# Long convolution beside a gated MLP: evictions issued one operation at a time between chunks, and a new spread of the chunks over the convolution's stages

## The chip, the cores and the metric

The kernel runs on one core of one Trainium2 chip. The metric is the device time of one execution in microseconds (us), the median of several runs. Comparisons use runs of the fast state. Engines are named as in the profile: PE is TensorE, PEld its weight loads, DVE VectorE, ACT ScalarE, POOL GpSimd, SP the queue that issues DMAs.

## The reference, cut to what matters

```python
# x, v: (4, 12480, 128); w_in: (128, 2048); w_out: (2048, 128); all float32
h_filt = (np.maximum(pos_emb @ w1, 0.0) @ w2) * np.exp(-0.01 * pos)[:, None]
u = x * v
y = irfft(rfft(u, n=2*S) * rfft(h_filt, n=2*S), n=2*S)[:, :S, :]    # along the sequence
z = (x * y).reshape(4 * 12480, 128)
h = z @ w_in
out = (h * np.cos(h)) @ w_out
```

## The kernel before

The FFTs are products with small DFT matrices. One sequence's convolution has five stages: **u** (product x*v, then sum and difference of mirrored rows, into the SBUF array `slots`; 30 units, no matmul), **f1** (first DFT factor, 64 units), **f2** (second factor and product with the filter, 48 units), **i1** (inverse, 64 units) and **i2** (30 units, times x, out to DRAM). The first sequence is convolved ahead (633 us, with the filter); the other three are convolved beside the MLP of the sequence before.

The MLP goes in *chunks*: 128 hidden columns for 480 tokens. A chunk is one up matmul, four element operations and one down matmul, spread over the engines (tile allocations are cut):

```python
    def moe_up(pool, n, c):                     # chunk i
        nc.tensor.matmul(ph[:, 0:TOK], w_in_sb[...], ats[n][:, :], start=True, stop=True)
        nc.scalar.activation(a, ph, AF.Identity, bias=quarter, scale=INV_TWO_PI)      # a
        nc.vector.tensor_scalar(out=k, in0=a, scalar1=ROUND, scalar2=ROUND, ...)      # k
        nc.gpsimd.tensor_tensor(f, a, k, op=ALU.subtract)                             # f
    def moe_act(pool, ph, f):                   # chunk i - 1
        nc.scalar.activation(cs, f, AF.Sin, scale=TWO_PI)                             # cs
        nc.vector.tensor_tensor(gt, ph, cs, op=ALU.mult)                              # gt
    def moe_down(n, c, gt):                     # chunk i - 4
        nc.tensor.matmul(accs[n][:, 0:TOK], w_out_sb[:, c, :], gt[:, :], ...)
    # ... cut ...
            owed += share                       # after each chunk, in the "gap":
            while owed > 0.0:                   # convolution work for `share` steps
                owed -= next(conv, owed)
```

The matmuls write to PSUM. Beside the MLP the program divides it into eight banks: two for `acc`, four for `ph`, **two for the convolution** (`cv`). FIFO (first in, first out) below means that an engine takes its instructions in the order in which they were issued. The convolution's units are issued by one generator; `steps` says for how many chunks a unit has to last, and `share` is the sum of steps over 380 chunks:

```python
    def units(n, steps, before, mm, after, ahead=2):
        # ... cut: loads ahead ...
        last = None
        for j in range(n):
            # ... cut ...
            now = mm(j)                  # takes a bank, issues the unit's matmuls
            if last is not None:
                after(j - 1, last)       # takes out the results of the unit before
            last = now
            yield steps
        after(n - 1, last)
        yield REST

    U_STEPS, F1_STEPS, F2_STEPS, I1_STEPS, I2_STEPS = 2.1, 1.2, 2.3, 1.2, 1.6

    def f1_evict(ps, b):
        pj = ps[:, 0:4 * N1].rearrange("p (i r k) -> p r k i", i=2, r=2)
        nc.scalar.copy(out=parts[0:ODD, :, :, b, :], in_=pj[0:ODD])
        nc.vector.tensor_copy(out=parts[ODD:KE, 0, :, b, :], in_=pj[ODD:KE, 1])
        nc.vector.tensor_scalar(out=parts[ODD:KE, 1, :, b, :], in0=pj[ODD:KE, 0],
                                scalar1=-1.0, scalar2=None, op0=ALU.mult)
    # i1_evict: one ScalarE copy, two VectorE operations; f2_product: four VectorE
    # multiplies from PSUM and two GpSimd additions; u: one product, one sum, one difference
```

Of the kernel before, what the change touches and what calls it, by code (L numbers as in the profile page):

```python
# [30 lines left out]
def kernel(  # L31
# [62 lines left out]
    UA = 2  # L94
# [174 lines left out]


# [57 lines left out]
    def u_multiply(tiles, engine):  # L328
        xt, vt = tiles
        engine.tensor_tensor(xt[:, :, :], xt[:, :, :], vt[:, :, :], op=ALU.mult)  # L330
# [9 lines left out]
    def f1_mm(ps, u, b):  # L340

        for i in range(2):
            nc.tensor.matmul(ps[0:KE, i * 2 * N1:(i + 1) * 2 * N1], u[:, b, 0:KE, i],  # L343
                             c1[0:u.shape[0], :, :].rearrange("p r k -> p (r k)"),
                             start=True, stop=True)

    def f1_evict(ps, b):
        pj = ps[:, 0:4 * N1].rearrange("p (i r k) -> p r k i", i=2, r=2)
        nc.scalar.copy(out=parts[0:ODD, :, :, b, :], in_=pj[0:ODD])
        nc.vector.tensor_copy(out=parts[ODD:KE, 0, :, b, :], in_=pj[ODD:KE, 1])  # L350
        nc.vector.tensor_scalar(out=parts[ODD:KE, 1, :, b, :], in0=pj[ODD:KE, 0],
                                scalar1=-1.0, scalar2=None, op0=ALU.mult)

    def f2_mm(ps, w, k1):

        for i in range(2):
            nc.tensor.matmul(ps[0:N2, i * 2 * D:(i + 1) * 2 * D], w[:, i, :],  # L357
                             parts[0:KE, :, k1 + i, :, :], start=True, stop=True)

    def f2_product(pool, ps, h, k1):  # L360
# [5 lines left out]
        for r, op in ((0, ALU.subtract), (1, ALU.add)):  # L366
            nc.vector.tensor_tensor(y[:, r], uu[:, 0], hh[:, r], op=ALU.mult)
            nc.vector.tensor_tensor(t[:, r], uu[:, 1], hh[:, 1 - r], op=ALU.mult)  # L368
            nc.gpsimd.tensor_tensor(y[:, r], y[:, r], t[:, r], op=op)  # L369

    def filter_keep(pool, ps, h, k1):

        uu = ps[0:N2, :].rearrange("p (g r d) -> p g r d", g=2, r=2)
        for g in range(2):
            k = slice(k1 + g, k1 + g + 1)
            nc.scalar.activation(h[:, g, :, :], uu[:, g, :, :], AF.Copy, scale=rot[:, 0, k])
            for r in range(2):
                nc.vector.scalar_tensor_tensor(
                    out=h[:, g, r, :], in0=uu[:, g, 1 - r, :], scalar=rot[:, 2 - r, k],
                    in1=h[:, g, r, :], op0=ALU.mult, op1=ALU.add)  # L380
        nc.sync.dma_start(hd[k1 // 2, :, :, :, :], h[:, :, :, :])

    def i1_mm(ps, b):
        for i in range(2):
            for r in range(2):
                nc.tensor.matmul(  # L386
                    ps[0:N1, (i * 2 + r) * N2:(i * 2 + r + 1) * N2],
                    parts[0:N2, r, :, b, i],
                    cs[:, r:r + 2, :].rearrange("p c a -> p (c a)"), start=True, stop=True)

    def i1_evict(pool, ps, b):
# [3 lines left out]
        for h, op in ((0, ALU.add), (1, ALU.subtract)):  # L395
            nc.vector.tensor_tensor(slots[0:N1, b, h * N2:(h + 1) * N2, :], pj[:, 0],  # L396
                                    other[:, :, :], op=op)

    def i2_mm(ps, t, g):
        for i in range(G):  # L400
# [9 lines left out]
    def i2_out(pool, ps, xs, b, g):  # L410
# [4 lines left out]
        nc.sync.dma_start(zd[b, :, g * G:(g + 1) * G, :], zs[:, :, :])  # L415

# [3 lines left out]
    def units(n, steps, before, mm, after, ahead=2):  # L420
        for j in range(min(ahead, n)):
            before(j)
        last = None
        for j in range(n):
            if j + ahead < n:
                before(j + ahead)
            now = mm(j)
            if last is not None:
                after(j - 1, last)
            last = now  # L430
            yield steps
        after(n - 1, last)
# [3 lines left out]
    U_STEPS, F1_STEPS, F2_STEPS, I1_STEPS, I2_STEPS = 2.1, 1.2, 2.3, 1.2, 1.6  # L436
# [3 lines left out]
    def u_units(b, bufs, u, engine, side="left"):  # L440
        with tc.tile_pool(name="xv", bufs=bufs, side=side) as pool:
# [5 lines left out]
            def mm(j):  # L447
                u_multiply(tiles[j], engine)
                return tiles.pop(j)

            clear_gap(u)
            yield from units(H // UA, U_STEPS, before, mm,
                             lambda j, t: u_sums(u, t, j * UA), ahead=bufs - 2)

    def f1_units(bank, u):
        def mm(j):
            ps = bank()
            f1_mm(ps, u, j)
            return ps

        return units(CB, F1_STEPS, lambda j: None, mm, lambda j, ps: f1_evict(ps, j))

    def f2_units(bank, use, make=None):

        with tc.tile_pool(name="there", bufs=2) as pool:
# [15 lines left out]
            def mm(j):  # L481
                ps = bank()
                f2_mm(ps, ws.pop(j), 2 * j)
# [303 lines left out]
```

## Time and profile before

The median of the first three runs is 4261 us (4259.9 to 4265.4). Mean lengths of the stages over the three sequences convolved beside the MLP, taken here and in all later tables from the first matmul of a stage to the first of the next (the end of i2 is its last matmul):

| | u | f1 | f2 | i1 | i2 | sum |
|---|---|---|---|---|---|---|
| measured, us | 150 | 176 | 268 | 186 | 133 | 914 |
| TensorE's floor, us | 107 | 171 | 227 | 182 | 135 | 822 |

The floor is what TensorE would need if it never waited: 1.663 us a chunk beside the stage, plus the stage's own matmuls. How these two figures come out of the profile is part of the prediction and stands there with its lines (its borders differ by 1 to 3 us, so that it has 916 for 914). The borders are read to about 2 us, and the u of the first of the three sequences is counted from 636 us. A chunk's own busy times on the other engines are below TensorE's: VectorE 1.2 us, GpSimd 1.22, ScalarE 1.3.

### The profile page before, as it was taken

The page shows a single profiled execution, that of the slowest core. Times are in us where ns is not written, and L with a number is a line of the kernel's source. Part 1 is how long each engine was busy: PE and PEld are TensorE (multiplying, and loading weights), DVE is VectorE, ACT ScalarE, POOL GpSimd, SP SyncE. Part 2 cuts the span into 40 slices and gives each one's busy share as a digit, 9 for nine tenths or more (in the row PEclk, how much of TensorE's full clock was granted, in tenths as well). Part 3 has the DMA queues.
Part 4 walks back from the last instruction along what each step waited for, and adds up shares of the span by engine and source line. Part 5 has one row for each costly group of instructions (what it writes and reads, how often), then busy time and mean ns, then how long its engine had stood idle before and what let it go on. Part 6 is the DMA issues. An engine that isn't in the chain of part 4 may idle for free.

```text
span 4262.5 us, 49170 instructions
## 1 busy us (share of the span) xinstructions
PE 3916.4 (92%) x13882; PEld 2244.3 (53%) x13882; DVE 3047.8 (72%) x6588; ACT 2415.2 (57%) x4484; POOL 2546.8 (60%) x2311
## 2 busy tenths in 40 slices
PE   5868778999999998998899989988999999999999
PEld 3836673554456653554466634644466644444444
DVE  8657669987778568777776588766675566666666
ACT  1343155775567445655455456644554577777777
POOL 2422347657865457568854476568754577777776
PEclk8557889999999999999999999999999999999999
DMA  3354343112211442012201531022103400000000
GB/s 86 89 167 120 96 136 106 50 52 78 82 51 42 142 142 85 15 50 81 75 12 51 177 112 42 15 73 78 52 15 107 127 19 19 19 19 19 19 19 14
DMA packets 271763, 293.63 MB, mean 69 GB/s; under 512 B 16741, under 2 KB 204101, under 8 KB 271237
## 3 DMA queue, kind: packets, MB, share of 16 engines
q1 hardware_dynamic: 271493, 290.50, 23.6%
q8 instruction: 112, 1.84, 0.2%
q14 instruction: 158, 1.29, 0.1%
HBM read 210.12 MB, written 80.31 MB: 68 GB/s over the span
## 4 chain that ended last, share of the span: by engine, by line
PE 65%; POOL 11%; DVE 10%; ACT 5%; DMA 5%; issue 3%; SPq 0%; DVEq 0%; POOLq 0%; ACTq 0%
PE ph L569 24%; PE acc L591 23%; POOL f L578 6%; POOL slots L369 5%; PE cv L404 4%; PE cv L386 4%; ACT cs L583 3%; PE cv L343 3%; PE ps L343 3%; DVE gt L585 2%; DMA w<-wd 2%; DMA hd<-h 2%; PE ph L116 2%; DVE slots L336 1%; PE ps L386 1%
## 5 line engine op out<-in xcount | busy, mean ns | idle before, releaser
L578 POOL TENSOR_TENSOR f<-a,k 128x480 f32<-128x480 f32 x1664 | 2021.9, 1218 | 1174.9 <-DVE k L575 1174.9
L569 PE MATMUL ph<-at,w_in_sb 128*128 128x480 f32 x3328 | 1647.4, 577 | 102.6 <-DVE gt L585 101.6
L591 PE MATMUL acc<-gt,w_out_sb 128*128 128x480 f32 x3328 | 1618.0, 568 | 0.5 <-DVE gt L585 0.5
L572 ACT ACTIVATE a<-ph,quarter 128x480 f32<-128x480 f32 x1664 | 1094.2, 658 | 750.7 <-PE ph L569 691.8
L585 DVE TENSOR_TENSOR gt<-ph,cs 128x480 f32<-128x480 f32 x1664 | 1091.7, 656 | 476.3 <-ACT cs L583 452.7
L583 ACT ACTIVATE cs<-f 128x480 f32<-128x480 f32 x1664 | 998.4, 600 | 690.6 <-POOL f L578 688.7
L575 DVE TENSOR_SCALAR k<-a 128x480 f32<-128x480 f32 x1664 | 778.8, 468 | 528.3 <-ACT a L572 514.4
L591 PEld LDWEIGHTS acc<-gt,w_out_sb 128*128 128x128 f32 x3328 | 633.8, 190 | 715.5 <-issue 713.5
L569 PEld LDWEIGHTS ph<-at,w_in_sb 128*128 128x128 f32 x3328 | 584.8, 191 | 575.4 <-issue 290.4
L369 POOL TENSOR_TENSOR slots<-slots,t 120x256 f32<-120x256 f32 x384 | 296.6, 795 | 228.2 <-DVE t L368 176.6
L357 PE MATMUL ps<-slots,w 124*120 124x256 f32 x384 | 165.9, 576 | 80.7 <-DVE w L250 45.6
L386 PEld LDWEIGHTS cv<-cs,slots 120*96 120x96 f32 x1536 | 180.5, 168 | 82.0 <-issue 72.1
L357 PE MATMUL cv<-slots,w 124*120 124x256 f32 x576 | 155.3, 390 | 49.7 <-PE acc L591 36.0
L404 PEld LDWEIGHTS cv<-slots,tm 96*104 96x104 f32 x1440 | 173.1, 171 | 46.7 <-issue 36.0
L386 PE MATMUL cv<-cs,slots 120*96 120x120 f32 x1536 | 191.2, 267 | 3.3 <-POOL slots L369 3.3
L404 PE MATMUL cv<-slots,tm 96*104 96x128 f32 x1440 | 178.7, 275 | 11.0 <-DMA tm<-td 7.2
L343 PEld LDWEIGHTS cv<-c,slots 104*124 104x124 f32 x768 | 130.6, 192 | 84.4 <-issue 54.8
L357 PEld LDWEIGHTS ps<-slots,w 124*120 124x120 f32 x384 | 93.0, 268 | 153.0 <-issue 70.5
L357 PEld LDWEIGHTS cv<-slots,w 124*120 124x120 f32 x576 | 98.7, 182 | 134.3 <-PE acc L591 78.0
L343 PE MATMUL cv<-c,slots 104*124 104x192 f32 x768 | 159.5, 330 | 3.2 <-POOL slots L336 2.6
L396 DVE TENSOR_TENSOR slots<-cv,other 96x240 f32<-96x240 f32 x384 | 135.9, 393 | 0.5
L330 POOL TENSOR_TENSOR xt<-xt,vt 104x512 f32<-104x512 f32 x30 | 38.3, 1276 | 137.5 <-DMA vt<-in_v_dram 127.0
(111 smaller groups left out, 2781.8 us busy)
## 6 DMA issues: line engine op xcount, KB each, us to landing
h<-hd SPq DMA_DIRECT2D x192, 240.0 KB
tm<-td SPq DMA_DIRECT2D x90, 312.0 KB
xt<-in_x_dram SPq DMA_DIRECT2D x120, 208.0 KB
vt<-in_v_dram SPq DMA_DIRECT2D x120, 208.0 KB
xs<-in_x_dram SPq DMA_DIRECT2D x120, 208.0 KB
zd<-zs SPq DMA_DIRECT2D x120, 208.0 KB
zb<-zd SPq DMA_DIRECT2D x104, 240.0 KB
out_dram<-ob SPq DMA_DIRECT2D x104, 240.0 KB
```

The lines of the kernel that those rows point to most:

```text
L343: nc.tensor.matmul(ps[0:KE, i * 2 * N1:(i + 1) * 2 * N1], u[:, b, 0:KE, i], c1[0:u.shape[0], :, :].rearrange("p r k -> p (r k)"), start=Tr ...
L357: nc.tensor.matmul(ps[0:N2, i * 2 * D:(i + 1) * 2 * D], w[:, i, :], parts[0:KE, :, k1 + i, :, :], start=True, stop=True)
L369: nc.gpsimd.tensor_tensor(y[:, r], y[:, r], t[:, r], op=op)
L386: nc.tensor.matmul(ps[0:N1, (i * 2 + r) * N2:(i * 2 + r + 1) * N2], parts[0:N2, r, :, b, i], cs[:, r:r + 2, :].rearrange("p c a -> p (c a) ...
L404: nc.tensor.matmul(ps[0:R, i * D:(i + 1) * D], t[:, i, r, :], slots[0:N1, :, place, :], start=(r == 0), stop=(r == 1))
L569: nc.tensor.matmul(ph[:, 0:TOK], w_in_sb[:, c * P:(c + 1) * P], ats[n][:, :], start=True, stop=True)
L572: nc.scalar.activation(a[:, :], ph[:, 0:TOK], AF.Identity, bias=quarter[:, 0:1], scale=INV_TWO_PI)
L575: nc.vector.tensor_scalar(out=k[:, :], in0=a[:, :], scalar1=ROUND, scalar2=ROUND, op0=ALU.add, op1=ALU.subtract)
L578: nc.gpsimd.tensor_tensor(f[:, :], a[:, :], k[:, :], op=ALU.subtract)
L583: nc.scalar.activation(cs[:, :], f[:, :], AF.Sin, scale=TWO_PI)
L585: nc.vector.tensor_tensor(gt[:, :], ph[:, 0:TOK], cs[:, :], op=ALU.mult)
L591: nc.tensor.matmul(accs[n][:, 0:TOK], w_out_sb[:, c, :], gt[:, :], start=(c == 0), stop=(c == NFC - 1))
```

## The change

The intent is to smooth the load. In u and f2, VectorE and GpSimd get a burst of operations in one gap and TensorE waits for the next chunk's elements. So evictions become generators that give up one operation per part of a unit, and the matmuls are halved too; and the steps move chunks from f1 and i1, where VectorE has little to do, to u and f2.

```diff
     def f1_evict(ps, b):
         nc.scalar.copy(out=parts[0:ODD, :, :, b, :], in_=pj[0:ODD])
         nc.vector.tensor_copy(out=parts[ODD:KE, 0, :, b, :], in_=pj[ODD:KE, 1])
+        yield
         nc.vector.tensor_scalar(out=parts[ODD:KE, 1, :, b, :], in0=pj[ODD:KE, 0],
                                 scalar1=-1.0, scalar2=None, op0=ALU.mult)
+        yield
 # ... the same in f2_product (4 parts), i1_evict (2), the product and the sums of u (3) ...
-    def units(n, steps, before, mm, after, ahead=2):
+    def units(n, steps, before, mm, after, parts, ahead=2):
-        last = None
+        last = iter(())
         for j in range(n):
             if j + ahead < n:
                 before(j + ahead)
-            now = mm(j)
-            if last is not None:
-                after(j - 1, last)
-            last = now
-            yield steps
-        after(n - 1, last)
+            now = None
+            for i in range(parts):
+                if i == 0 or 2 * i == max(parts, 2):
+                    now = mm(j, now, min(i, 1))
+                if i == 0 and parts == 1:
+                    now = mm(j, now, 1)
+                next(last, None)
+                yield steps / parts
+            next(last, None)
+            last = after(j, now)
+        for _ in last:
+            pass
         yield REST
-    U_STEPS, F1_STEPS, F2_STEPS, I1_STEPS, I2_STEPS = 2.1, 1.2, 2.3, 1.2, 1.6
+    U_STEPS, F1_STEPS, F2_STEPS, I1_STEPS, I2_STEPS = 3.2, 0.6, 3.25, 0.6, 1.6
 # ... cut: a third of the i2 twiddles made on GpSimd in both places where they are made
 #     (before, a quarter in one); the first sequence's u issued in thirds of a unit, at three times as many places ...
```

More of the change, by code (lines that the diff above doesn't have):

```diff
@@ L268, in make_t, with make_third @@
              tw_t[:, 1, n2:n2 + 1], **how)
+    def make_third(pool, t, n2, half=None):
+        if n2 % 3 < 2:
+            make_t(t, n2, half=half)
+        else:
+            spare = pool.tile([N1, 2, R], F32, name="spare")
+            make_t(t, n2, spare=spare[:, :, :])
     ROWS = 8
@@ L326, in u_load, with u_multiply @@
         return tiles
-    def u_multiply(tiles, engine):
+    def u_multiply(tiles, half, engine):
         xt, vt = tiles
-        engine.tensor_tensor(xt[:, :, :], xt[:, :, :], vt[:, :, :], op=ALU.mult)
+        engine.tensor_tensor(xt[:, half, :], xt[:, half, :], vt[:, half, :], op=ALU.mult)
     def u_sums(u, tiles, a):
@@ L337, in u_sums, with f1_mm @@
                             below, above, op=op)
-    def f1_mm(ps, u, b):
-        for i in range(2):
-            nc.tensor.matmul(ps[0:KE, i * 2 * N1:(i + 1) * 2 * N1], u[:, b, 0:KE, i],
-                             c1[0:u.shape[0], :, :].rearrange("p r k -> p (r k)"),
-                             start=True, stop=True)
+    def f1_mm(ps, u, b, i):
+        nc.tensor.matmul(ps[0:KE, i * 2 * N1:(i + 1) * 2 * N1], u[:, b, 0:KE, i],
+                         c1[0:u.shape[0], :, :].rearrange("p r k -> p (r k)"),
+                         start=True, stop=True)
     def f1_evict(ps, b):
@@ L350, in f1_evict, with f2_mm @@
         nc.vector.tensor_copy(out=parts[ODD:KE, 0, :, b, :], in_=pj[ODD:KE, 1])
+        yield
         nc.vector.tensor_scalar(out=parts[ODD:KE, 1, :, b, :], in0=pj[ODD:KE, 0],
                                 scalar1=-1.0, scalar2=None, op0=ALU.mult)
-    def f2_mm(ps, w, k1):
-        for i in range(2):
-            nc.tensor.matmul(ps[0:N2, i * 2 * D:(i + 1) * 2 * D], w[:, i, :],
-                             parts[0:KE, :, k1 + i, :, :], start=True, stop=True)
+        yield
+    def f2_mm(ps, w, k1, i):
+        nc.tensor.matmul(ps[0:N2, i * 2 * D:(i + 1) * 2 * D], w[:, i, :],
+                         parts[0:KE, :, k1 + i, :, :], start=True, stop=True)
     def f2_product(pool, ps, h, k1):
@@ L367, in f2_product @@
             nc.vector.tensor_tensor(y[:, r], uu[:, 0], hh[:, r], op=ALU.mult)
+            yield
             nc.vector.tensor_tensor(t[:, r], uu[:, 1], hh[:, 1 - r], op=ALU.mult)
             nc.gpsimd.tensor_tensor(y[:, r], y[:, r], t[:, r], op=op)
+            yield
     def filter_keep(pool, ps, h, k1):
@@ L380, in filter_keep, with i1_mm @@
                     in1=h[:, g, r, :], op0=ALU.mult, op1=ALU.add)
+            yield
         nc.sync.dma_start(hd[k1 // 2, :, :, :, :], h[:, :, :, :])
-    def i1_mm(ps, b):
-        for i in range(2):
-            for r in range(2):
-                nc.tensor.matmul(
-                    ps[0:N1, (i * 2 + r) * N2:(i * 2 + r + 1) * N2],
-                    parts[0:N2, r, :, b, i],
-                    cs[:, r:r + 2, :].rearrange("p c a -> p (c a)"), start=True, stop=True)
+    def i1_mm(ps, b, i):
+        for r in range(2):
+            nc.tensor.matmul(
+                ps[0:N1, (i * 2 + r) * N2:(i * 2 + r + 1) * N2],
+                parts[0:N2, r, :, b, i],
+                cs[:, r:r + 2, :].rearrange("p c a -> p (c a)"), start=True, stop=True)
     def i1_evict(pool, ps, b):
@@ L397, in i1_evict, with i2_mm @@
                                     other[:, :, :], op=op)
-    def i2_mm(ps, t, g):
-        for i in range(G):
+            yield
+    def i2_mm(ps, t, g, part):
+        for i in range(part * G // 2, (part + 1) * G // 2):
             n2 = g * G + i
@@ L415, in i2_out @@
         nc.sync.dma_start(zd[b, :, g * G:(g + 1) * G, :], zs[:, :, :])
-    def units(n, steps, before, mm, after, ahead=2):
+        yield
+    def units(n, steps, before, mm, after, parts, ahead=2):
         for j in range(min(ahead, n)):
             before(j)
-        last = None
+        last = iter(())
         for j in range(n):
@@ L445, in before, with after, mm @@
                 tiles[j] = u_load(pool, bufs, b, j * UA)
-            def mm(j):
-                u_multiply(tiles[j], engine)
-                return tiles.pop(j)
+            def after(j, _):
+                for half in range(2):
+                    u_multiply(tiles[j], half, engine)
+                    yield
+                u_sums(u, tiles.pop(j), j * UA)
+                yield
             clear_gap(u)
-            yield from units(H // UA, U_STEPS, before, mm,
-                             lambda j, t: u_sums(u, t, j * UA), ahead=bufs - 2)
+            yield from units(H // UA, U_STEPS, before, lambda j, ps, i: None, after, 3,
+                             ahead=bufs - 2)
     def f1_units(bank, u):
-        def mm(j):
-            ps = bank()
-            f1_mm(ps, u, j)
+        def mm(j, ps, i):
+            if i == 0:
+                ps = bank()
+            f1_mm(ps, u, j, i)
             return ps
-        return units(CB, F1_STEPS, lambda j: None, mm, lambda j, ps: f1_evict(ps, j))
+        return units(CB, F1_STEPS, lambda j: None, mm, lambda j, ps: f1_evict(ps, j), 2)
     def f2_units(bank, use, make=None):
@@ L479, in before, with mm @@
                     nc.sync.dma_start(hs[j][:, :, :, :], hd[j, :, :, :, :])
-            def mm(j):
-                ps = bank()
-                f2_mm(ps, ws.pop(j), 2 * j)
+            def mm(j, ps, i):
+                if i == 0:
+                    ps = bank()
+                f2_mm(ps, ws[j], 2 * j, i)
                 return ps
             yield from units(N1 // 2, F2_STEPS, before, mm,
-                             lambda j, ps: use(pool, ps, hs.pop(j), 2 * j))
+                             lambda j, ps: use(pool, ps, hs.pop(j), 2 * j),
+                             4 if use is f2_product else 2)
     def i1_units(bank):
         with tc.tile_pool(name="mid", bufs=2) as pool:
-            def mm(j):
-                ps = bank()
-                i1_mm(ps, j)
+            def mm(j, ps, i):
+                if i == 0:
+                    ps = bank()
+                i1_mm(ps, j, i)
                 return ps
             yield from units(CB, I1_STEPS, lambda j: None, mm,
-                             lambda j, ps: i1_evict(pool, ps, j))
+                             lambda j, ps: i1_evict(pool, ps, j), 2)
     def i2_units(bank, b, make=None):
@@ L512, in before, with mm @@
                                   block(x, b, slice(j * G, (j + 1) * G)))
-            def mm(j):
-                ps = bank()
-                i2_mm(ps, ts.pop(j), j)
+            def mm(j, ps, i):
+                if i == 0:
+                    ps = bank()
+                i2_mm(ps, ts[j], j, i)
                 return ps
             yield from units(N2 // G, I2_STEPS, before, mm,
-                             lambda j, ps: i2_out(pool, ps, xss.pop(j), b, j))
+                             lambda j, ps: i2_out(pool, ps, xss.pop(j), b, j), 2)
     def t_units():
@@ L527, in t_units @@
                 for i in range(G):
-                    make_t(t[:, i, :, :], g * G + i)
+                    make_third(pool, t[:, i, :, :], g * G + i)
                     yield
@@ L535, in conv_units @@
         keep = t_units() if b == 1 else iter(())
-        for steps in f1_units(bank, slots[0:R, :, :, :]):
-            next(keep, None)
+        for i, steps in enumerate(f1_units(bank, slots[0:R, :, :, :])):
+            if i % 2:
+                next(keep, None)
             yield steps
         yield from f2_units(bank, f2_product)
-        for steps in i1_units(bank):
-            next(keep, None)
+        for i, steps in enumerate(i1_units(bank)):
+            if i % 2:
+                next(keep, None)
             yield steps
@@ L667 @@
             for j, _ in enumerate(f1_units(bank, slots[0:FR, :, :, :])):
-                if j % 4 == 3:
+                if j % 8 > 4:
                     next(first_u, None)
@@ L671 @@
                     bank, filter_keep, lambda w, k1: make_w(w, k1, half=bank))):
-                if j % 3 == 2:
+                if j % 2:
                     next(first_u, None)
@@ L690 @@
             with tc.tile_pool(name="spare", bufs=2) as pool:
-                def make(t, n2):
-                    if n2 % G < G - 1:
-                        make_t(t, n2, half=bank)
-                    else:
-                        spare = pool.tile([N1, 2, R], F32, name="spare")
-                        make_t(t, n2, spare=spare[:, :, :])
-                for _ in i2_units(bank, 0, make):
+                for _ in i2_units(bank, 0, lambda t, n2: make_third(pool, t, n2, bank)):
                     pass
```

## The prediction

> **What bounds the kernel now.** I first asked for the busy time of each engine between the stage borders (the first and last matmul of each convolution stage on TensorE). Columns: start:end and length in us, then busy us and instruction count of TensorE, weight loads, VectorE, ScalarE, GpSimd, then clock and DMA. The rows are sequence 2's stages u (input product), f1, f2, i1 with i2 together, and the end without convolution:
>
> ```profile
> 1546.00:1695.60 149.60, 123.34 (x297) 50.29 (x295) 132.19 (x201) 79.22 (x136) 111.07 (x98) 0.99 0.35 102
> 1695.60:1869.10 173.50, 172.76 (x604) 102.52 (x604) 129.78 (x294) 116.16 (x224) 93.77 (x78) 1.00 0.07 19
> 1869.10:2134.60 265.50, 239.56 (x696) 121.86 (x696) 188.41 (x428) 133.66 (x230) 213.19 (x207) 1.00 0.27 77
> 2134.60:2458.00 323.40, 319.37 (x1556) 207.66 (x1556) 202.78 (x427) 167.30 (x325) 153.02 (x128) 0.99 0.27 80
> 3380.50:4262.00 881.50, 876.28 (x2369) 424.05 (x2367) 607.45 (x1119) 668.53 (x1085) 633.20 (x526) 1.00 0.07 19
> ```
>
> TensorE is full except in u and f2. The chain that ended last says the same: in the end, in f1 and in i1 it is matmuls alone; in f2 (1000 to 1200 us) it is not:
>
> ```profile
> by line: POOL slots L369 27.8%; POOL f L578 25.8%; ACT cs L583 10.7%; DVE gt L585 10.6%; issue 5.5%; DVE t L368 5.5%; PE ph L569 5.4%; PE acc L591 4.1%; DVE slots L367 1.5%; DVE at L564 1.3%; DVE k L575 0.9%; PE cv L357 0.9%; PE ph L116 0.2
> ```
>
> A busy TensorE is not a full one, so I take its pace from that chain in the end: 0.805 us for the up matmul, 0.805 for the down matmul, and two sets of transposes (0.44 and 0.41) in 16 chunks, together **1.663 us a chunk**. Check: 524 chunks are left there, 871 us, and 881.5 are seen. Convolution work on TensorE, from starts in the timeline: f1 0.65 us a unit (64 units), f2 0.88 (48), i1 0.82 (64), i2 1.77 (30). The chunks beside a stage are its steps over the share (382.5/380 = 1.0066). Mean of the three sequences, floor against measured: u 64.1 chunks = 107, measured 149; f1 77.8 chunks + 42 = 171, 176; f2 111.2 chunks + 42 = 227, 268; i1 77.8 + 52 = 182, 187; i2 49.2 + 53 = 135, 136. **TensorE loses 94 us a sequence, 83 of them in u and f2.** That is what the change goes for.
>
> **What the Trainium skill says.**
> - "PSUM — Partial Sum Buffer", section "Engine vs sequencer instructions": the queues of ScalarE, VectorE and GpSimd are strict FIFO, and matmuls keep program order. The trace agrees: below, VectorE reaches a convolution operation only behind k and gt of its chunk.
> - "SBUF — State Buffer", section "SBUF: two separate sides": VectorE operations with two SBUF inputs and GpSimd exclude each other on a shared port. The trace agrees: the subtraction of u takes 410 ns at best and 947 in the median (beside GpSimd's addition).
> - "Perfetto Trace Analysis", section "Identifying Performance Opportunities": TensorE's busy share is no measure of headroom, and the same gap repeating can mean too few PSUM buffers. The first agrees: at 1.663 us a chunk the matmuls of the end are called 99% busy, yet every chunk's time is theirs. The second is what I expect of the new kernel.
>
> **The change, part by part.** No matmul is added or taken away. Steps go to 3.2 (u), 0.6 (f1, i1), 3.25 (f2); 384.3 in all, share 1.0113, so the end without convolution stays as it is. Chunks beside each stage: u 96.4, f1 39.5, f2 155.7, i1 39.5, i2 48.9.
>
> u: floor 160 us. VectorE has per chunk k 0.468, gt 0.656 and 0.083 of copies, and per unit 1.75 of product and difference (the product now in two halves): 3.2 x 1.207 + 1.8 = 5.66 busy against TensorE's 5.32. Overlapping ends and the port waits inflate these: consecutive starts show k at 0.4 and gt at 0.57 when nothing delays them, which makes 5.1. TensorE should be about the bound; with 8 us of slips, **168**.
>
> f2: floor 155.7 x 1.663 + 42 = 301. A chunk now meets one VectorE multiply (0.416) and at most one GpSimd addition (0.8): GpSimd per unit 3.25 x 1.22 + 1.59 = 5.55 of TensorE's 6.29. Loose enough. Where the last multiply of a unit and the first matmul of the unit after next fall in one gap between chunks (I counted 10 a sequence from the step sizes), the matmul waits for its bank, 1.8 us by the slot below: 18. With 4 of slips, **323**.
>
> f1 and i1 are the dear part. Convolution has two PSUM banks. A unit's first matmul needs the bank of two units ago, whose last eviction operation is issued **just one part earlier**. Before, a unit took 1.2 steps, so a chunk lay between; now a part takes 0.3, so three or four parts fall into one gap, and the eviction and the matmul waiting for it lie in the same gap. The order of the changed instructions shows it: of 38 gaps in f1 some 23 have three parts and 14 have four, and each has at least one bank wait inside. How far behind is VectorE? From the timeline of before (start, duration, engine, line):
>
> ```profile
> 1698.64 0.97 PE L569 MATMUL ph<-at,w_in_sb 128*128 128x480 f32 x2
> ...
> 1699.45 0.97 PE L591 MATMUL acc<-gt,w_out_sb 128*128 128x480 f32 x2
> ...
> 1699.65 0.66 ACT L572 ACTIVATE a<-ph,quarter 128x480 f32<-128x480 f32 x1 [0.37 <-PE ph L569]
> 1699.90 0.35 DVE L351 TENSOR_SCALAR slots<-cv 60x192 f32<-60x192 f32 x1
> 1700.20 0.59 ACT L583 ACTIVATE cs<-f 128x480 f32<-128x480 f32 x1
> ...
> 1700.41 0.41 DVE L575 TENSOR_SCALAR k<-a 128x480 f32<-128x480 f32 x1 [0.16 <-ACT a L572]
> ...
> 1700.85 0.66 DVE L585 TENSOR_TENSOR gt<-ph,cs 128x480 f32<-128x480 f32 x1
> ...
> 1701.52 0.36 DVE L350 COPY slots<-cv 60x192 f32<-60x192 f32 x1
> ...
> 1701.81 0.35 DVE L351 TENSOR_SCALAR slots<-cv 60x192 f32<-60x192 f32 x1
> ```
>
> From the start of the up matmul, the first eviction operation starts at 2.88 us and the second ends at 3.52, behind a, k, cs and gt. TensorE passes the same place at 1.61. The trace already has one case in which TensorE waits for that second operation, ending 866.38; the matmul starts 0.15 later (I use 0.12, the weight load's start). The profile names another engine there, so this reading is mine:
>
> ```profile
> 866.03 0.35 DVE L351 TENSOR_SCALAR slots<-cv 60x192 f32<-60x192 f32 x1
> ...
> 866.50 0.63 PEld L343 LDWEIGHTS cv<-c,slots 104*124 104x124 f32 x4 [0.86 <-ACT a L572]
> 866.53 0.89 PE L343 MATMUL cv<-c,slots 104*124 104x192 f32 x4
> ```
>
> So a gap of f1 with parts (first, second, first) goes: matmuls to 2.26, wait until 3.64, end 3.97. Starting with the second part: ready 1.94, wait until 3.35, end 4.00. Four parts: 4.29 or 4.33. By the counts (12, 11, 8, 6) that is 152 us, plus 2.3 and 2 for the partial gaps, 1 for the rest and 3 for the transposes' copies in VectorE's queue: **160**, floor 107. In i1 the parts are 0.41 and the evictions 0.33 apart, 0.39 long: 4.13, 4.21, 4.54, 4.62, in the same way **168**, floor 118. The stall is about 1.4 us in each of 75 gaps, 103 us a sequence, where 10 were lost before.
>
> i2: unchanged, 135. Before the MoE phase (633 us) the order on each engine is nearly the same, and the chain there is DMA stores, waits and matmuls; the larger GpSimd share of the twiddles hides beside the stores of zs (58% of that chain). I give it 0.
>
> Sum per sequence: 168 + 160 + 323 + 168 + 135 = 954 against 916 measured before: +38. Three sequences: +114; 4261 + 114 = **4375 us**.
>
> **Rivals.**
> - The intent holds: u and f2 give back their stalls and f1 and i1 lose 10 as before. Then 94 falls to 41 (8 + 22 + 10 + 1 of i2): 4261 - 3 x 53 = 4102. For it: f1 and i1 have spare VectorE time on average (130 of 173 us). Against it: an average doesn't move an operation that stands behind gt in a FIFO; the wait is by order, not by load.
> - Bank waits as I say, and u and f2 without any stall: 4375 - 3 x 30 = 4285, still no gain. Bank waits with u and f2 stalled half as much as before: 4375 + 3 x 12 = 4411.
> - Bank waits a quarter shorter (ScalarE or VectorE earlier than in my slot): 4375 - 3 x 26 = 4297.
> - The halves of the product and the port make VectorE the bound of u at 5.66 a unit: 30 units, 170, only 2 more.
>
> **Range and chances.** The bank wait is forced by order and its length is read from one slot; the residual stalls of u and f2 are the weaker figures, and they lean upward. Range 4305 to 4450. For a gain of over 2% (under 4176) the waits would have to be absent: 0.03. Within 2% (to 4346) takes shorter waits or clean u and f2 stages: 0.25. Slower: 0.72.
>
> **What would show it.** In f1 and i1 of the new profile: idle of TensorE before the convolution matmuls or their weight loads, 1.2 to 1.5 us per gap, ended by VectorE's evictions (or named as ScalarE); stages of about 160 and 168 us, TensorE's granted pace unchanged. In f2 the GpSimd addition should leave the chain, the stage near 323; u near 168. Wrong if f1 takes about 110 us (no wait), or if f2 stays 40 above its floor. The end stays 880.

## The result, and the profile after

The changed kernel took **4541.8 us** (median of four runs, 4540.2 to 4542.5) against 4261.7 for the kernel before on the same chip. The ratio is **1.0655** (95% interval 1.0637 to 1.0674). Ratios here are the mean time of one kernel's fast runs over that of the other's in the same rounds, so not quite the ratio of the medians. The result is correct.

The direction and the bank wait came as predicted; the size did not: +280 us against +114 predicted, outside the range. Busy times between the stage borders of the second of the three sequences, in the kernel after (columns: start:end, length, busy us of PE, PEld, DVE, ACT, POOL, then clock and DMA; the fourth row is i1 and i2 together, the last is the end without convolution):

```profile
1648.00:1843.70 195.70, 178.13 (x440) 74.91 (x438) 186.44 (x300) 116.77 (x202) 151.60 (x129) 1.00 0.30 83
1843.70:2007.50 163.80, 115.51 (x428) 72.09 (x429) 83.91 (x211) 72.73 (x145) 47.84 (x40) 1.00 0.05 13
2007.50:2349.50 342.00, 316.07 (x897) 159.00 (x897) 248.88 (x525) 195.92 (x323) 263.62 (x252) 0.99 0.23 63
2349.50:2654.00 304.50, 260.98 (x1384) 177.29 (x1385) 157.23 (x342) 122.51 (x243) 105.27 (x88) 0.99 0.28 82
3660.00:4540.00 880.00, 875.42 (x2365) 424.00 (x2363) 604.33 (x1116) 667.77 (x1082) 631.60 (x525) 1.00 0.07 19
```

In f1 nothing is busy: TensorE 115 of 164 us, VectorE 84. That is what a wait by order looks like, in contrast to a load. u is the opposite, VectorE busy 186 of 196 (the profile counts a held-up operation as busy: the product of u takes 923 ns in the median and 411 at best). The clock is granted in full, and the end takes 880 us as before, so the throttle plays no part.

| mean of three sequences, us | u | f1 | f2 | i1 | i2 | sum |
|---|---|---|---|---|---|---|
| before | 150 | 176 | 268 | 186 | 133 | 914 |
| predicted after | 168 | 160 | 323 | 168 | 135 | 954 |
| measured after | 199 | 165 | 339 | 172 | 131 | 1007 |

Three times 1007 - 914 is 279 of the 280 us. Of these, 8 stand before the MLP (its first up matmul starts at 642.5 us, before at 634.8) and are counted in the first u; from each run's own start u is 198, before 151. Against the prediction, u is 31 us too long a sequence (30 from its own start) and f2 16; f1 and i1 are off by 5 and 4.

**f1.** The waits of the kernel after (who waited for whom: us in total, times, longest) begin, among those of the convolution's matmuls, with the two whose bank was asked for too early. In the kernel before no line of the list has a convolution matmul waiting for these evictions:

```profile
PE cv L350 <- DVE slots L359: 130.7, 104, 1.6
...
PE cv L396 <- DVE slots L406: 120.4, 110, 1.4
```

That is 251 us. (The weight loads of the same matmuls are listed as waiting for ScalarE's copies. In the gap below, these end at 1904.22, 0.6 us before VectorE's operation, which is therefore the one that counts.) One gap of f1 in the timeline (start, duration, engine, line, tile; in brackets the idle time before and what ended it):

```profile
1901.28 0.97 PE L598 MATMUL ph<-at,w_in_sb 128*128 128x480 f32 x2
...
1902.09 0.97 PE L620 MATMUL acc<-gt,w_out_sb 128*128 128x480 f32 x2
1902.29 0.66 ACT L601 ACTIVATE a<-ph,quarter 128x480 f32<-128x480 f32 x1 [2.52 <-PE ph L598]
...
1902.89 0.81 PE L350 MATMUL cv<-c,slots 104*124 104x192 f32 x4
...
1903.06 0.41 DVE L604 TENSOR_SCALAR k<-a 128x480 f32<-128x480 f32 x1 [2.10 <-ACT a L601]
1903.34 0.88 ACT L356 COPY slots<-cv 64x384 f32<-64x384 f32 x2
1903.50 0.66 DVE L614 TENSOR_TENSOR gt<-ph,cs 128x480 f32<-128x480 f32 x1
...
1904.17 0.36 DVE L357 COPY slots<-cv 60x192 f32<-60x192 f32 x1
1904.45 0.35 DVE L359 TENSOR_SCALAR slots<-cv 60x192 f32<-60x192 f32 x1
...
1904.95 0.89 PE L350 MATMUL cv<-c,slots 104*124 104x192 f32 x4 [1.24 <-DVE slots L359]
```

Counted from the up matmul at 1901.28: the first eviction operation starts at 2.89 us (predicted 2.88), the second ends at 3.52 (3.52), the waiting matmul starts at 3.67 (3.64). ScalarE and VectorE stand idle for over 2 us before a and k, because the next up matmul is behind the waiting convolution matmul in TensorE's queue. So all engines wait for one another in turn.

**u.** The chain that ended last, in a stretch of u of the kernel after, shares by line:

```profile
by line: POOL f L607 36.9%; POOL slots L344 17.2%; issue 12.0%; ACT cs L612 10.5%; DVE gt L614 8.9%; DVE k L604 7.1%; DVE xt L338 2.7%; ACT a L601 1.2%; PE ph L598 1.1%; PE acc L620 0.9%; DVE ob L633 0.8%; DVE at L593 0.7%; DVEq L604 0.0%; 
```

TensorE has 2% of it. One gap in the timeline that holds a product half (L338):

```profile
1747.16 1.20 POOL L607 TENSOR_TENSOR f<-a,k 128x480 f32<-128x480 f32 x1 [0.68 <-DVE k L604]
1747.72 0.92 DVE L338 TENSOR_TENSOR xt<-xt,vt 104x256 f32<-104x256 f32 x1
...
1748.57 0.40 DVE L604 TENSOR_SCALAR k<-a 128x480 f32<-128x480 f32 x1
...
1749.04 1.20 POOL L607 TENSOR_TENSOR f<-a,k 128x480 f32<-128x480 f32 x1 [0.68 <-DVE k L604]
```

The product half, 0.41 us at best in this run, is started while GpSimd's f runs and ends 0.28 us after f. The next k stands behind it in VectorE's queue, and the next f needs that k. The gap lasts 1.88 us: f, the end of the product, k, in turn. TensorE would need 1.66. The chain names GpSimd most; whether that is GpSimd's own load or the port is asked by e8, e10 and e11.

**f2.** The gain is there in part: GpSimd's addition has 0.7% of the chain between the borders above, and matmuls have nine tenths. What remains has a mark, waits of about 2 us before a convolution matmul: in the three sequences 30 of over 1.2 us, ten in each, as the prediction had counted; they last 1.5 to 2.3 us, 1.87 in the mean, 19 us a sequence. One of the longer ones in the chain (start, length, what), which names no releaser for it:

```profile
2171.87 0.82 PE acc L620 x2
2172.69 2.15 issue
2174.84 0.67 PE cv L365 x2
```

The timeline has the last multiply of the unit two before, which ends at 2174.74, and the matmul:

```profile
2174.32 0.42 DVE L377 TENSOR_TENSOR t<-cv,h 120x256 f32<-120x256 f32 x1
...
2174.84 0.67 PE L365 MATMUL cv<-slots,w 124*120 124x256 f32 x2 [2.16 <-issue]
```

It is the same bank wait. All 30 waits end 0.10 us after the end of an L377.

### The profile page after: what moved, and what is told of

It is laid out like the page before. It is cut to its first block, busy times and chain, and to the rows that moved or that the text cites. A ratio compares the mean times of both kernels' runs of the same rounds, so it can differ in the third digit from the quotient of the medians.

```text
span 4540.7 us, 49216 instructions
## 1 busy us (share of the span) xinstructions
PE 3961.9 (87%) x13882; PEld 2246.0 (49%) x13882; DVE 3099.7 (68%) x6628; ACT 2449.8 (54%) x4484; POOL 2617.4 (58%) x2441
## 4 chain that ended last, share of the span: by engine, by line
PE 63%; DVE 13%; POOL 7%; ACT 7%; issue 6%; DMA 4%; DVEq 0%; POOLq 0%; SPq 0%; ACTq 0%
PE ph L598 24%; PE acc L620 20%; POOL f L607 5%; PE cv L415 4%; DVE gt L614 3%; ACT a L601 3%; PE cv L365 3%; PE cv L396 3%; DVE k L604 3%; PE ps L350 3%; PE cv L350 2%; POOL slots L344 2%; ACT cs L612 2%; DMA hd<-h 1%; DMA w<-wd 1%
## 5 line engine op out<-in xcount | busy, mean ns | idle before, releaser
L607 POOL TENSOR_TENSOR f<-a,k 128x480 f32<-128x480 f32 x1664 | 2001.4, 1203 | 1468.7 <-DVE k L604 1468.7
L604 DVE TENSOR_SCALAR k<-a 128x480 f32<-128x480 f32 x1664 | 718.2, 432 | 907.5 <-ACT a L601 887.8
L378 POOL TENSOR_TENSOR slots<-slots,t 120x256 f32<-120x256 f32 x384 | 311.4, 817 | 153.8 <-DVE t L377 144.8
L396 PE MATMUL cv<-cs,slots 120*96 120x120 f32 x1536 | 203.3, 271 | 126.3 <-DVE slots L406 120.4
L350 PE MATMUL cv<-c,slots 104*124 104x192 f32 x768 | 173.9, 341 | 149.0 <-DVE slots L359 130.7
L365 PE MATMUL cv<-slots,w 124*120 124x256 f32 x576 | 182.9, 398 | 70.2 <-issue 56.5
L338 DVE TENSOR_TENSOR xt<-xt,vt 104x256 f32<-104x256 f32 x180 | 186.6, 1038 | 0.0
```

The source lines that it names most:

```text
L350: nc.tensor.matmul(ps[0:KE, i * 2 * N1:(i + 1) * 2 * N1], u[:, b, 0:KE, i], c1[0:u.shape[0], :, :].rearrange("p r k -> p (r k)"), start=Tr ...
L365: nc.tensor.matmul(ps[0:N2, i * 2 * D:(i + 1) * 2 * D], w[:, i, :], parts[0:KE, :, k1 + i, :, :], start=True, stop=True)
L378: nc.gpsimd.tensor_tensor(y[:, r], y[:, r], t[:, r], op=op)
L396: nc.tensor.matmul(ps[0:N1, (i * 2 + r) * N2:(i * 2 + r + 1) * N2], parts[0:N2, r, :, b, i], cs[:, r:r + 2, :].rearrange("p c a -> p (c a) ...
L604: nc.vector.tensor_scalar(out=k[:, :], in0=a[:, :], scalar1=ROUND, scalar2=ROUND, op0=ALU.add, op1=ALU.subtract)
L607: nc.gpsimd.tensor_tensor(f[:, :], a[:, :], k[:, :], op=ALU.subtract)
```

## The experiments

Theory **Order**: TensorE loses its time in f1, i1 and part of f2 because a bank is asked for in the same gap in which its last reader was just issued, behind k and gt in VectorE's FIFO. Theory **Port**: u is held by the turns that VectorE and GpSimd take on their shared SBUF port. Rival to both, **Load**: the stages last as long as their busiest engine has work, plus what the extra instructions cost. Twelve kernels ran. Stage means over three sequences, from the traces (us):

| run | steps u, f1, f2, i1 | u | f1 | f2 | i1 | i2 | time, us |
|---|---|---|---|---|---|---|---|
| before | 2.1 1.2 2.3 1.2 | 150 | 176 | 268 | 186 | 133 | 4262 |
| after | 3.2 0.6 3.25 0.6 | 199 | 165 | 339 | 172 | 131 | 4542 |
| e1 split only | 2.1 1.2 2.3 1.2 | 151 | 216 | 282 | 223 | 135 | 4541 |
| e2 steps only | 3.2 0.6 3.25 0.6 | 202 | 147 | 330 | 158 | 131 | 4426 |
| e3 own bank | 3.2 0.6 3.25 0.6 | 198 | 110 | 340 | 122 | 132 | 4226 |
| e4 f2 late | 3.2 0.6 3.25 0.6 | 199 | 166 | 314 | 173 | 132 | 4472 |
| e5 product on ScalarE (wrong result) | as after | 188 | 165 | 339 | 172 | 132 | 4509 |
| e6 product on GpSimd | as after | 206 | 166 | 338 | 172 | 132 | 4562 |
| e7 both repairs | 3.2 0.6 3.25 0.6 | 199 | 111 | 314 | 122 | 131 | 4152 |
| e8 product from PSUM (wrong result) | as after | 185 | 165 | 340 | 172 | 133 | 4504 |
| e9 both repairs, old steps | 2.1 1.2 2.3 1.2 | 149 | 176 | 242 | 184 | 134 | 4175 |
| e10 and difference from PSUM (wrong) | as after | 178 | 165 | 339 | 172 | 133 | 4483 |
| e11 and sum off GpSimd (wrong) | as after | 170 | 166 | 340 | 172 | 132 | 4459 |
| e12 both repairs, more beside u | 4.7 0.6 2.3 0.6 | 271 | 111 | 237 | 121 | 134 | 4143 |

e5, e6, e8, e10 and e11 are single runs with a profile (state unknown); their stages are read, their times only support them. In each, the four stages that the edit does not touch stay within 2 us of the kernel after, so they serve as the control.

### e1: the split alone

```diff
-    U_STEPS, F1_STEPS, F2_STEPS, I1_STEPS, I2_STEPS = 3.2, 0.6, 3.25, 0.6, 1.6
+    U_STEPS, F1_STEPS, F2_STEPS, I1_STEPS, I2_STEPS = 2.1, 1.2, 2.3, 1.2, 1.6
```

> The changed kernel with the old steps (2.1, 1.2, 2.3, 1.2, 1.6): the split alone. Order theory (TensorE waits for a convolution bank whose eviction lies in the same gap between chunks): parts of 0.6 steps, so some 26 of 77 gaps of f1 and of i1 hold a second part followed by a first part, 1.4 us each: f1 207 us, i1 218. f2 with parts of 0.575: some 20 gaps with the last part followed by a first, 2.1 us each: 270. u about 152, i2 136. Sum 983 a sequence against 916 before: 4460 us. Rival (load of the engines alone sets the stages): the chunks beside each stage are those of before, so 4261.

Measured: 4540.8 us, ratio to before 1.0646 (1.0629 to 1.0664). f1 216, i1 223, f2 282, u 151, within 12 us of what Order said; f1, i1 and f2 are all longer than expected, and the total is 81 us over the 4460 of the expectation. Load is refuted: with the old spread of chunks the split by itself costs 280 us. That this total equals that of the full change is chance, for the loss lies in other stages. Splitting the bursts of f2 did not help f2 here; it went from 268 to 282. Its trace has 61 waits of over 1.2 us before f2's matmuls, 20 a sequence as expected, 37 us a sequence.

### e2: the steps alone

```diff
 # on the kernel before
-    U_STEPS, F1_STEPS, F2_STEPS, I1_STEPS, I2_STEPS = 2.1, 1.2, 2.3, 1.2, 1.6
+    U_STEPS, F1_STEPS, F2_STEPS, I1_STEPS, I2_STEPS = 3.2, 0.6, 3.25, 0.6, 1.6
```

> The kernel before with the new steps (3.2, 0.6, 3.25, 0.6, 1.6): the new spread of chunks alone, evictions in one piece. Order theory: 26 of 38 gaps of f1 and i1 hold two units, the second waits 1.4 us for the eviction just issued: f1 143, i1 152. u by the sum of what takes the port shared by VectorE and GpSimd (3.2 x 1.53 + 1.75): 196. f2 about 320, i2 134. Sum 945: 4350 us. Rival (load): u and f2 relieved, f1 and i1 full, 4100.

Measured: 4426.1 us, ratio 1.0381 (1.0366 to 1.0397); the expectation was 4350. The stages but i2 came out 4 to 10 us above it, u at 202 for 196. The pattern is Order's again: two whole units in one gap are enough for a bank wait, f1 147 over its floor of 107. The split makes it worse (165), as a first part behind a second part occurs in every gap.

### e3: a unit's own eviction right behind its matmuls, in f1 and i1

```diff
 # units(..., own=False); f1 and i1 beside chunks: parts 1, own=True, steps unchanged
                 if i == 0 and parts == 1:
                     now = mm(j, now, 1)
+                if own:
+                    for _ in after(j, now):
+                        pass
                 next(last, None)
 ...
-            last = after(j, now)
+            last = iter(()) if own else after(j, now)
```

The idea: VectorE reaches the gap more than a microsecond behind TensorE, so the unit's matmuls are done when the eviction's turn comes. There was no need to lag by a unit, and without the lag a bank is free one gap sooner.

> The changed kernel, but in f1 and i1 beside chunks a unit is one part and its own eviction is issued right behind its matmuls, so that a bank is asked for again a gap later. Order theory: no bank waits in f1 and i1; f1 from 165 to about 110 us (floor 107), i1 from 173 to about 121 (floor 118): 4541 - 3 x 107 = 4220 us. Rival (f1 and i1 are slow because VectorE and ScalarE have more evictions per chunk to do): same work per chunk, nothing changes, 4541.

Measured: 4225.8 us, ratio 0.9912 (0.9897 to 0.9927); expected 4220. f1 fell from 165 to 110 and i1 from 172 to 122. Same operations, same steps, same two banks: only the order differs. (It differs in two ways, as the halves of a unit are put together again too. e2 has whole units with the lag and 147 and 158 us, so the missing lag is worth 37 and 36 us, the halves the rest.) **Order is shown for f1 and i1, and it is worth 316 us of the changed kernel's time.** The chain in f1 is matmuls alone again (a stretch of f1, shares by line):

```profile
by line: PE cv L350 37.1%; PE ph L601 30.2%; PE acc L623 29.8%; PE ph L116 2.1%; PE cv L365 0.9%
```

### e4: the matmuls of f2 one part later

```diff
+                if parts == 4:
+                    if i % 2:
+                        now = mm(j, now, i // 2)
-                if i == 0 or 2 * i == max(parts, 2):
+                elif i == 0 or 2 * i == max(parts, 2):
                     now = mm(j, now, min(i, 1))
```

> The changed kernel, but in the product stage f2 the two matmuls of a unit stand in its second and fourth part instead of its first and third, so the bank is asked for two parts after the last read of it, not one. Order theory: the waits of about 2.1 us in f2 (10 or more a sequence) vanish, f2 from 339 to about 312 us: 4541 - 3 x 27 = 4460. Rival (f2 is held by VectorE and GpSimd time): f2 stays at 339, 4541.

Measured: 4472.0 us, ratio to before 1.0490 (1.0475 to 1.0506), f2 from 339 to 314 (expected 4460 and 312). Of the 30 waits three are left, of 1.3 us. So the bank wait cost f2 25 of the 38 us that it lay above its floor of 301: 19 as the waits themselves, and some 6 that went with them, which nothing here explains. The remaining 13 are probably VectorE's and GpSimd's, which hold about a seventh of the chain there; no run takes them apart.

### e5 and e6: the product of u on another engine

```diff
 # e5: wrong result on purpose
-        engine.tensor_tensor(xt[:, half, :], xt[:, half, :], vt[:, half, :], op=ALU.mult)
+        nc.scalar.activation(xt[:, half, :], xt[:, half, :], AF.Copy, scale=vt[:, half, 0:1])
 # e6: right result
-        yield from u_units(b, 4, slots[0:R, :, :, :], nc.vector)
+        yield from u_units(b, 4, slots[0:R, :, :, :], nc.gpsimd)
```

> Wrong result on purpose: in stage u beside chunks the product of two SBUF tensors on VectorE is replaced by a scaled copy on ScalarE, which takes nothing of the port shared by VectorE and GpSimd. Port theory (f 1.2, k 0.33, product halves 0.35 each, difference 0.33 and sum 0.73 take turns on one port): u per unit 3.2 x 1.53 + 1.06 = 5.96 us, 179 us a sequence instead of 196, 4490 us. Rival (VectorE's own queue and load set u): VectorE falls to 4.8 us a unit, below TensorE's 5.32, u at its floor of 160, 4433.

> The product of stage u goes from VectorE to GpSimd, result right. Port theory: the product halves now hold the port 0.73 us each instead of 0.35, u per unit 3.2 x 1.53 + 3 x 0.73 + 0.33 = 7.4 us, 222 us a sequence instead of 196, 4620 us. Rival (VectorE's load sets u): VectorE is relieved by 0.8 us a unit and more and u falls to 160 to 181, 4430 to 4500.

Measured: u 188 with the product on ScalarE, 206 with it on GpSimd, against 199. That VectorE's load holds u is refuted by e6, in which VectorE is relieved and u grows. But both Port numbers (179 and 222) were missed by half of the effect or more. In e5 the copies took a place in the chain themselves: ScalarE's next a stood behind them, 6.8% of u's chain. In e6 the chain is GpSimd's operations one after another, and k slips in between at the edges, so that adding whole durations counts too much. These two runs settle the direction and not the size; and as e6 keeps GpSimd busy for 201 of the 206 us, it can't tell the port from GpSimd's own load. A cleaner edit was needed.

### e8, e10, e11: taking u off the port step by step

```diff
 # e8: one initialised PSUM bank is held through u; wrong result on purpose
-    ... vt[:, half, :], op=ALU.mult)
+    ... held[0][0:R, half * UA * D:(half + 1) * UA * D], op=ALU.mult)
 # e10: also the difference's second operand from PSUM
 # e11: also the sum as a copy on ScalarE instead of an addition on GpSimd
```

The number and size of VectorE's operations stay the same in all three; only where they read from changes. GpSimd's stay the same in e8 and e10; e11 takes the sum away from it.

> Wrong result on purpose: in stage u beside chunks the product on VectorE has the same count and size, but takes its second factor from PSUM instead of SBUF, so it no longer needs the port shared with GpSimd. Port theory: the product halves shrink from 0.92 us and more to about 0.42, u from 198 to about 175 us a sequence, 4470 us. Rival (VectorE's number of operations and its queue set u): u stays at 195 to 199, 4535 to 4545.

> Wrong result on purpose: as the run with the product's second factor in PSUM, and the difference of stage u takes its second operand from PSUM too, so that of u's work only GpSimd's sum uses the shared port. Taking away the product's port use moved u from 199 to 185 us a sequence. Port theory: the difference holds the port about 0.3 us a unit, so u falls by some 9 more, to 176, and what stays above the floor of 160 is the sum and the turns of f and k: 4475 us. Rival (VectorE's queue alone makes the rest): u stays at 185, 4502.

> Wrong result on purpose: as before, and the sum of stage u goes from GpSimd to a copy on ScalarE: nothing of u uses the shared port, VectorE has the same operations as in the changed kernel. Port theory: u near its floor, 160 to 166 us a sequence, 4440 us. Rival (VectorE's operations in its queue hold u): u at 175 to 185, 4475 to 4500.

Measured: u 199, then 185, 178, 170 us (from each run's own first up matmul 198, 186, 178, 169). **Port is shown for the product and the difference:** both engines did the same operations, and u lost 21 us (20 from the own starts) as these two left the port, about 12 and 8. Neither VectorE's load nor GpSimd's explains that. The last 8 or 9 us, for the sum, are the port or the place that it had in GpSimd's queue; e11 changes both, and no run separates them. The product and the difference in u, first of the kernel after, then of e8 (engine, operation, tile, count, then min/median/max in ns):

```profile
L338 DVE TENSOR_TENSOR xt<-xt,vt x180: 411/923/1478, 652.2 to 2849.1; 104x256 f32<-104x256 f32 x180
...
L344 DVE TENSOR_TENSOR slots<-xt x90: 416/922/1022, 655.7 to 2849.6; 104x256 f32<-104x256 f32 x90
```

```profile
L343 DVE TENSOR_TENSOR xt<-xt,cv x180: 404/410/415, 646.0 to 2809.2; 104x256 f32<-104x256 f32 x180
L349 DVE TENSOR_TENSOR slots<-xt x90: 425/747/1083, 649.2 to 2809.6; 104x256 f32<-104x256 f32 x90
```

With a PSUM operand the product takes 404 to 415 ns every time, beside the same f. In e10 the difference does the same (408 to 419 ns), and GpSimd's sum beside it falls from 1232 ns in the median to 897. The sizes were not all met: e8 was expected at 175, the difference at 9, e11 at 160 to 166. Its 170 leave 10 us over the floor of 160, near the 8 that the prediction had allowed for slips.

### e7, e9, e12: the repairs together

e7 is e3 and e4 in one; e9 is the same with the old steps (2.1, 1.2, 2.3, 1.2, 1.6); e12 the same with 4.7, 0.6, 2.3, 0.6, 1.6.

> The changed kernel with both repairs: f1 and i1 as in the own-bank run, f2 as in the late-matmul run. If the bank waits are the whole of what those stages lost and the two repairs do not touch each other, u 198, f1 110, f2 314, i1 122, i2 131, 875 us a sequence: 4148 us, 2.7% under the kernel before. If the waits only move to another stage: 4226, as with the first repair alone.

> Both repairs, but the old steps (2.1, 1.2, 2.3, 1.2, 1.6). If the new spread of chunks earns nothing because u is held by the port whatever stands beside it, and f2 needs only the evictions spread out: u 150, f1 172, f2 237, i1 183, i2 134, 876 us a sequence, 4150 us, the same as with the new steps. If the spread is worth what the change meant by it, this run is slower than the one with the new steps by 50 us and more.

> Both repairs with steps 4.7, 0.6, 2.3, 0.6, 1.6: chunks moved from f2 to u. Between the two repaired runs a chunk beside u cost 49 us / 33 = 1.47 us and one beside f2 72 / 44.5 = 1.62. Moving 44.5 chunks: u about 264, f2 242, f1 111, i1 122, i2 131, 870 a sequence against 876: 4131 us. If u's cost per chunk rises to TensorE's 1.663 by then: 4150 to 4155, no gain.

Measured: e7 4151.6 us, ratio to before **0.9741** (0.9728 to 0.9754), expected 4148: the two repairs add up. e9 4174.7, ratio 0.9800 (0.9787 to 0.9813): the repairs with the old spread give 86 us and the new spread only 23 more. It is half way between the two expectations (equal, or 50 us and more). In e9, f2 fell to 242 from 268, and is 40 below e1's 282, whose bank waits took 37: there, spreading the evictions pays, once no bank wait eats it. e12 4142.9, ratio 0.9722 (0.9709 to 0.9736), the fastest, but its interval overlaps with that of e7. Its u cost 72 us for 45 more chunks, 1.61 each, where 1.47 had been hoped for.

## Why the prediction was wrong

Point by point, by the steps of its sum (us a sequence):

- **Pace of TensorE, floors, the end without convolution:** held. The end took 880 us; with the waits repaired f1 took 110 (floor 107) and i1 122 (118).
- **f1 and i1, bank waits in the gap:** held in cause and nearly in size. 165 and 172 measured, 160 and 168 predicted; the slot agrees to 0.03 us. e3 shows the cause.
- **f2, "with 4 of slips, 323":** the bank wait was right in count and length (ten of 1.87 us, 19 us a sequence; predicted ten of 1.8, 18). The slips were the term that was too small: 339 - 301 - 19 leaves 19 and not 4. Of these e4 takes away 6 together with the waits, and 13 stay. At 38 us above its floor, f2 came close to the prediction's own sign of being wrong (40).
- **u, "TensorE should be about the bound; with 8 us of slips, 168":** this is the step that failed, 31 us a sequence, 93 of the 167 us by which the total was missed (a few of these stand before the MLP, see below). I had looked at the port, and quoted the skill on it, but added its cost to VectorE's time alone and then chose the undisturbed figures (5.1 us a unit). In u neither engine is the bound by itself: f, k, product, difference and sum take turns on one port (k too: its median in the second sequence's u is 397 ns, and 804 in e6, where GpSimd is never free), and k stands behind the product in VectorE's FIFO. A gap with a product half takes 1.88 us, the one with sum and difference 2.35 (from the start of one f to that of the next in the timeline), together 6.1 for three chunks where TensorE needs 5.0; a unit has 3.2 chunks and took 6.6. e8 and e10 show that about 20 of the 31 are the port's; another 8 went in e11 with the sum, by the port or by GpSimd's queue.
- What the change could not get in u: from 64 to 96 chunks, u went from 150 to 199 us (149 to 199 from e9 to e7, which differ in the steps alone), so what it lies above its floor stayed, 43 and 39. More chunks hid u's own work no better. That this is because each chunk brings its own f and k to the port is likely, but not shown.
- **i2:** held, 131 for 135. **The part before the MLP**, "I give it 0", cost 8 us in the profiles (first up matmul at 642.5, before at 634.8). In the other runs that keep the split it lies anywhere from 635.2 to 642.5; why is open.
- One reading shows less than the prediction says. In the end without convolution TensorE is 99% busy and the chain is all matmuls, so there the busy share does not mislead; u shows the point, where TensorE is busy for 123 us and needs 107.
- The rival "u is bound by VectorE at 5.66, only 2 more" was the nearest to the truth and was cut down to the wrong size. The range had no room for it, as its upper end rested on u being within a few microseconds of TensorE.

The change's own reasoning failed in f1 and i1: these have spare VectorE *time*, and it was taken for room to pack more units between two chunks. With two banks, and a unit's eviction a unit behind, one gap can start about one unit. Above their floors, u and f2 lost 4 and 3 us less a sequence than before, and f1 and i1 together 112 where it had been 9.

## What to carry to other kernels

Before packing more work between two fixed points of an in-order stream, ask when each buffer was last read, in gaps and not in operations: an eviction that is issued just ahead of the matmul that needs its bank makes TensorE wait for everything that stands ahead of it in the other engine's queue. Try a smaller lag first; issuing a unit's own eviction at once cost nothing here and freed the bank one gap sooner. And where VectorE operations that read SBUF alone run beside GpSimd's, add up what both put on the shared port as if it were one engine, as an upper estimate (e6); an operand in PSUM took two of them off it here (e8, e10).

## What the Trainium skill lacked or had wrong

- "SBUF — State Buffer", section "SBUF: two separate sides": right that the loser of the port blocks (923 ns in the median for a product that takes 410 when one operand is in PSUM). But taking the port as held for an instruction's whole duration in the profile overstates: for the product on GpSimd (e6), the expectation's sum gives 3 x 1.53 + 3 x 0.73 + 0.33 = 7.1 us for a unit of three chunks, and from one GpSimd sum to the next such a unit takes 6.37 in the timeline.
- "Perfetto Trace Analysis", section "Identifying Performance Opportunities": repeated gaps as a sign of too few PSUM buffers is the right sign here (251 us before the convolution matmuls of f1 and i1), but the cure needed no buffer: with the same two banks and another order of issue the gaps went, 316 us.
- No page read says how far an engine that keeps FIFO order lags behind TensorE in a software-pipelined stream; here it is 2.9 us from the start of the up matmul to the first eviction operation, against 1.6 us for TensorE, and that number set the bank wait in f1 and i1.
